# Ring slots at another offset, the last operands of h kept in the ring, weight sums and decodes at other steps, attention's head in another order

## The chip, the cores and the metric

The program runs on one core of a Trainium2 chip. TensorE (PE; its weight loads PEld) multiplies, VectorE (DVE), ScalarE (ACT) and GpSimd (POOL) work elementwise, SyncE (SP) issues transfers; ACT and POOL issue some too. The metric is the time of one execution in device microseconds; three runs of the kernel before gave 886.06, 886.5 and 888.85 us, a median of 886.5 us.

## The reference

Three stages, all float32. First a decayed linear attention over 4 batches of 8 heads, 768 positions of 64 features:

```
for t in range(S):
    state = gamma * state + k[t]^T v[t]          # 64 x 64 per head
    y[t]  = scale * q[t] state
```

Its output, 3072 tokens of 512 features, goes through `h = ((x @ w1) * (x @ w2)) @ w3; x = h @ w_out` (512 to 1024 to 1024 to 512), and then through `h = max(x @ w1, x @ w2, x @ w3); out = h @ w_out` (512 to 768 to 512). The weights reach the chip as 64-bit floats.

## The kernel before

**Operands and products.** Every 64-bit weight tile is fetched into one of three staging tiles (`stg`), decoded by a chain of short operations (ACT L113, POOL L115, DVE L136 and L138, ACT L145, then DVE L130 into `wraw`, or DVE L124 and ACT L126 for weights without sums) and split into a high and a low part, `w_q`. A product takes three matmuls of 128x512: high by high, high by low, low by high (L449 to L451, L559 to L561, L634 to L636, L690 to L692). ACT's cast and DVE's subtraction (`split_to`, L220 and L221) make the two parts of the moving operands in the same way.

**Seven products.** The products of stages B (x by w1 and w2, L449) and H (x by w1, w2, w3 of the last layer, L634) are done by a seven-product scheme on 2x2 blocks. One step q = 0..6 multiplies one operand (a sum of blocks of x, made by `op_pre`) with one weight set `w_q` (a sum of blocks of the weight, made by `weights`). A step of B has 24 matmuls, one of H has 18. B has 2 groups of 3 blocks of 7 steps (42), H has 3 columns j of 3 blocks (63). Operand s lies in ring slot `op_t[s % 4]`. In B's first group the operands are made in the ring and stored to DRAM (`opsp`); B's second group and H load them back, three steps ahead, with a DMA that POOL issues (L441, L538). Between B and H lie the merge of w3 with w_out (L498 to L500) and a stage M (L559), 24 steps, that makes x2, the input of H. H's operands are made by `gen(n, q)`: those of blocks 0 and 1 during M, those of block 2 during column 0 of H, at its steps 1, 2, 4, 5, 7, 8 and 10, through two tiles `gen0` and `gen1` and `opsp`.

**What sets the order.** The order of instructions is written out by hand; each engine runs its own in order. `Spread(jobs, slots)` deals out side jobs: at tick t it has run ceil(jobs x t / slots) of them. A tick comes after each quarter of a B step or third of an H step. One `step` is half a decode. `wgen(q)` writes `w_q` of the next group during the last block of the present one, one per step; its sums run on POOL (L197 to L199 at q = 2, L201 at q = 6), its split on ACT and DVE (L204, L205). In attention the decodes, a drain and the seven `wgen` are dealt over two ticks per chunk.

**Attention.** 24 chunks of 128 positions: `scores` (PE L293, then DVE's mask product L295 into `a`), `attn_av` (L311), `attn_st` (L322, state copied by ACT L326), `attn_in` (L302), `attn_ev` (DVE L331). `scale_v` (POOL L283) scales v in place two chunks ahead. A chunk is loaded in two halves, 512 KB each, into four slots `ck`.

Of the kernel before, what the change touches and what calls it, by code (L numbers as in the profile page):

```python
# [46 lines left out]
def fused_kernel(ctx: ExitStack, tc: tile.TileContext, ck, w12, w3t, wo1, w123, wo2, mask, gout, kdec, out):  # L47
# [107 lines left out]
    def drain():  # L155
        while loaded or fronts or mids or lows or pending or phase[0]:
            step()
        due_more()

    later = []  # L160

# [29 lines left out]
    def weights(raw, n):  # L191
        tmp = s_t[:, :n]

        def emit(q):
            r0, r1, r2, r3 = raw
            if q == 2:
                nc.gpsimd.tensor_tensor(out=tmp, in0=r2, in1=r3, op=ALU.add)  # L197
                nc.gpsimd.tensor_tensor(out=r2, in0=r2, in1=r0, op=ALU.subtract)
                nc.gpsimd.tensor_tensor(out=r0, in0=tmp, in1=r0, op=ALU.subtract)  # L199
            elif q == 6:  # L200
                nc.gpsimd.tensor_tensor(out=r1, in0=r1, in1=r0, op=ALU.subtract)  # L201
            src = (r0, r1, r0, r2, tmp, r3, r1)[q]
            w = wslot(q, n)
            nc.scalar.copy(out=w[:, 0], in_=src)  # L204
            nc.vector.tensor_tensor(out=w[:, 1], in0=src, in1=w[:, 0], op=ALU.subtract)  # L205

        return emit

    def raw_quads(n):
        return [wraw_t[0][:, i * n:(i + 1) * n] for i in range(4)]  # L210

    def op_slot(s):
        return op_t[s % 4][:, :].rearrange("p (h k n) -> p h k n", h=2, k=2)

    def view2(t):
        return t.rearrange("p (k n) -> p k n", k=2)
# [11 lines left out]
    def t_buf(n):  # L228
        return view2(work["T"][:, n % 2 * 1024:n % 2 * 1024 + 1024])

# [118 lines left out]

    with tc.manual_schedule():  # L350
        nc.sync.dma_start(out=mask_sb, in_=mask)
        load_half(0, 0)
        nc.sync.dma_start(out=kdec_sb, in_=kdec)
        load_half(0, 1)
        nc.sync.dma_start(out=gout_sb[:, 0], in_=gout[:, 0])
        load_half(1, 0)
        load_half(1, 1)
        for b in range(2):
            nc.gpsimd.memset(st_sb[b], 0.0)
# [12 lines left out]
        ops_b = {}  # L372
        side = Spread([step] * (4 * GA) + [drain] + [lambda q=q: wgen(q) for q in range(7)], 2 * (last - 3))
        for i in range(last + 1):
            attn_in(i)
            scores(i + 1)
            if i > 1:
                side.tick()
            attn_av(i)
            scale_v(i + 2)  # L380
            attn_st(i)
            attn_ev(i)
            if i > 1:
                side.tick()
            load_half(i + 4, 0)
            if i < 2:
                more()
                if i == 1:
                    more()
                    nc.sync.dma_start(out=gout_sb[:, 2:], in_=gout[:, 2:])  # L390
            load_half(i + 4, 1)
            if i == last - 2:
                op_split(0, quad_b(0)(0, 0))
# [4 lines left out]
        for nm in ("U", "C", "E", "T"):  # L398
            work[nm] = b_pl.tile([P, 2048], F32, name=nm)
        b_pl.tile([P, 8], F32, name="pad_b")  # L400
        op_split(1, quad_b(0)(1, 0))
# [3 lines left out]
        for g in range(KF // GA):  # L405
            if g == 0:
                wq += [lambda i=i, u=u: fetch_w12(i, u) for i in range(GA, KF) for u in range(2)]
                more(3)
                side = Spread([step] * (4 * GA), 2 * 28 + 4)
            else:  # L410
# [8 lines left out]
                more(3)  # L419
                side = Spread([step] * 32, 3 * 28)  # L420
            wgen = weights(raw_quads(1024), 1024)
# [121 lines left out]
        f_load(5)  # L543
        side = Spread([step] * (4 * GH), 18)
        wgen = weights(raw_quads(256 * GH), 256 * GH)
# [32 lines left out]
        g_st, g_pl = stage_pool("g")  # L578
        gen_t = [g_pl.tile([P, 2048], F32R, name=f"gen{z}") for z in range(2)]
        h_st, h_pl = stage_pool("h", "right")  # L580
# [16 lines left out]
        for j in range(GH):  # L597
# [3 lines left out]
            if j + 1 < GH:  # L601
                wq += [lambda w=w, u=u: fetch_w123(j + 1, w, u) for w in range(GH) for u in range(2)]
                side = Spread([step] * (4 * GH), 2 * 21 + 3)
            else:
                o_st, o_pl = stage_pool("o")
                wo2_sb = [o_pl.tile([P, 2, 512], F32R, name=f"wo2_{k}") for k in range(KH)]
                hop0 = o_pl.tile([P, 2, 1536], F32R, name="hop0")
                hop = [(hop0[:, 0], hop0[:, 1]), (w_t[0][:, :1536], w_t[1][:, :1536]), (w_t[2][:, :1536], w_t[3][:, :1536])]
                wq += [lambda k=k: fetch(wo2[k], None, wo2_sb[k][:, 0], wo2_sb[k][:, 1]) for k in range(KH)]
                side = Spread([step] * (2 * KH) + [drain], 2 * 21)  # L610
            more(3)
            wgen = weights(raw_quads(256 * GH), 256 * GH)
            for n in range(NB):
# [3 lines left out]
                for q in range(7):  # L617
                    s = 7 * blk + q
                    op_load(s + 3)
                    if s in (1, 2, 4, 5, 7, 8, 10):  # L620
                        gen(NB - 1, (1, 2, 4, 5, 7, 8, 10).index(s))
                    if j == GH - 1 and n == NB - 1 and q == 3:
# [4 lines left out]
                    which, first = ORDER[q]  # L627
                    x = op_slot(s)
                    w = wslot(q, 256 * GH).rearrange("p h (i k n) -> p h i k n", i=GH, k=2)
# [126 lines left out]
```

## Time and profile before

| | |
|---|---|
| median of 3 runs | 886.5 us |
| profiled execution, its own time | 884.03 us |
| its span, first to last instruction | 882.2 us |
| PE busy | 859.2 us (97%) |
| PE's weight loads busy | 709.7 us (80%) |
| DVE, ACT, POOL busy | 542.7, 344.2, 224.0 us |
| moved by DMA | 243.61 MB, 276 GB/s on average |

Busy times of PE contain modelled ends of pipelined matmuls, so that 97% says that PE rarely stands still, not how fast it goes. How fast it goes is read as the time of a stretch divided by its matmuls. All times below are microseconds from the start of the span.

### The profile page before, as it was taken

The numbers are of one execution on the slowest core, as the hardware profiler recorded it, in microseconds if no ns is written. First come the engines' busy times: TensorE is split into PE (matmuls) and PEld (weight loads), VectorE is DVE, ScalarE is ACT, GpSimd is POOL, SyncE is SP. The second block draws the span as 40 slices with busy tenths as digits, with TensorE's granted clock in tenths as the row PEclk, the third lists the DMA queues.
The fourth block names the chain that finished last, engine by engine and source line by source line (L and its number), as shares of the span: only waits on it lengthen the run. The fifth ranks groups of instructions, "written<-read, shape, count | busy, mean of one in ns | idle before, by whom it ended". The sixth has DMA issues, their size and how long they took to land. (4 is left out here: it accounts for less than half of the span.)

```text
span 882.2 us, 12037 instructions
## 1 busy us (share of the span) xinstructions
PE 859.2 (97%) x4614; PEld 709.7 (80%) x4614; DVE 542.7 (62%) x682; ACT 344.2 (39%) x530; POOL 224.0 (25%) x228
## 2 busy tenths in 40 slices
PE   8988999999999999999999999899999999999998
PEld 7877888888788888888888887688888778888886
DVE  2797969798485756752575577566656676351220
ACT  1333364543345343633554463343323342233231
POOL 2437215175242422100201232142214221000000
PEclk9999999999999999999999999999999999999999
DMA  9998277867799977453485599999998999965431
GB/s 336 408 379 266 97 291 281 345 251 284 279 324 355 323 255 278 143 210 120 170 286 242 211 402 411 417 330 344 375 325 269 314 359 343 305 203 178 153 118 63
DMA packets 63464, 243.61 MB, mean 276 GB/s; under 512 B 6320, under 2 KB 15664, under 8 KB 47152
## 3 DMA queue, kind: packets, MB, share of 16 engines
q1 hardware_dynamic: 45120, 132.23, 40.4%
q0 software_dynamic: 12096, 88.09, 28.3%
q10 hardware_dynamic: 6192, 22.55, 7.0%
q8 instruction: 36, 0.59, 0.3%
q14 instruction: 20, 0.16, 0.1%
HBM read 170.48 MB, written 72.35 MB: 275 GB/s over the span
## 5 line engine op out<-in xcount | busy, mean ns | idle before, releaser
L634 PE MATMUL bank<-op,w 128*128 128x512 f32 x378 | 149.6, 396 | 5.6 <-DVE m L652 2.0
L636 PE MATMUL bank<-op,w 128*128 128x512 f32 x378 | 148.2, 392 | 0.0
L635 PE MATMUL bank<-op,w 128*128 128x512 f32 x378 | 147.0, 389 | 0.0
L449 PE MATMUL bank<-op,w 128*128 128x512 f32 x336 | 132.5, 394 | 0.7 <-ACT U L454 0.7
L451 PE MATMUL bank<-op,w 128*128 128x512 f32 x336 | 131.6, 392 | 0.0
L450 PE MATMUL bank<-op,w 128*128 128x512 f32 x336 | 130.7, 389 | 0.0
L115 POOL TENSOR_SCALAR dec<-dec 128x512 f32<-128x512 f32 x64 | 46.6, 728 | 302.1 <-ACT dec L113 289.7
L634 PEld LDWEIGHTS bank<-op,w 128*128 128x128 f32 x378 | 71.0, 188 | 22.8 <-ACT E L643 3.1
L636 PEld LDWEIGHTS bank<-op,w 128*128 128x128 f32 x378 | 70.9, 188 | 16.6
L635 PEld LDWEIGHTS bank<-op,w 128*128 128x128 f32 x378 | 71.0, 188 | 15.5
L559 PE MATMUL bank<-op,w 128*128 128x512 f32 x192 | 75.6, 394 | 0.0
L561 PE MATMUL bank<-op,w 128*128 128x512 f32 x192 | 75.2, 392 | 0.0
L449 PEld LDWEIGHTS bank<-op,w 128*128 128x128 f32 x336 | 63.1, 188 | 14.6 <-ACT U L454 1.5
L451 PEld LDWEIGHTS bank<-op,w 128*128 128x128 f32 x336 | 63.1, 188 | 14.6
L560 PE MATMUL bank<-op,w 128*128 128x512 f32 x192 | 74.6, 389 | 0.0
L450 PEld LDWEIGHTS bank<-op,w 128*128 128x128 f32 x336 | 63.1, 188 | 13.8
L113 ACT ACTIVATE dec<-stg 128x512 f32<-128x512 f32 x64 | 42.5, 665 | 66.9 <-DMA stg<-in_wo_dram 32.1
L538 POOL DMA_DIRECT2D op<-opsp x63 | 34.6, 550 | 129.0 <-PE bank L636 103.7
L145 ACT ACTIVATE dec<-stg 128x512 int32<-128x512 uint32 x64 | 43.1, 673 | 56.8 <-DVE stg L138 56.6
L136 DVE TENSOR_SCALAR dec<-dec 128x512 int32<-128x512 int32 x64 | 37.0, 578 | 44.2 <-POOL dec L115 44.2
L138 DVE SCALAR_TENSOR_TENSOR stg<-stg,dec 128x512 int32<-128x512 int32 x64 | 46.7, 729 | 5.1 <-DVE dec L136 0.4
L465 POOL TENSOR_TENSOR C<-C,U 128x512 f32<-128x512 f32 x24 | 37.3, 1574 | 25.6 <-DVE C L464 25.6
(128 smaller groups left out, 1525.9 us busy)
## 6 DMA issues: line engine op xcount, KB each, us to landing
op<-opsp POOLq DMA_DIRECT2D x84, 1024.0 KB, 8.1
ck<-in_ck_dram SPq DMA_DIRECT2D x48, 512.0 KB, 7.1
opsp<-op SPq DMA_DIRECT2D x21, 1024.0 KB, 5.7
opsp<-w SPq DMA_DIRECT2D x14, 1024.0 KB, 4.9
stg<-in_w_dram ACTq DMA_DIRECT2D x19, 512.0 KB, 6.5
hsp<-m SPq DMA_DIRECT2D x36, 256.0 KB, 7.0
stg<-in_w3t_dram ACTq DMA_DIRECT2D x16, 512.0 KB, 4.3
stg<-in_w_dram SPq DMA_DIRECT2D x15, 512.0 KB, 9.6
```

The costliest lines, as they stand in the source:

```text
L115: nc.gpsimd.tensor_scalar(out=df, in0=df, scalar1=MAX_HI, scalar2=MIN_HI, op0=ALU.min, op1=ALU.max)
L138: nc.vector.scalar_tensor_tensor(out=top, in0=top, scalar=-0x40000000, in1=dec, op0=ALU.bitwise_and, op1=ALU.bitwise_or)
L145: nc.scalar.activation(out=dec, in_=low.bitcast(U32), func=ACT.Copy, scale=2.0 ** -29)
L449: nc.tensor.matmul(ps, wh, x[:, 0, k, :], start=first and k == 0, stop=False, skip_group_check=True)
L450: nc.tensor.matmul(ps, wh, x[:, 1, k, :], start=False, stop=False, skip_group_check=True)
L451: nc.tensor.matmul(ps, wl, x[:, 0, k, :], start=False, stop=k == 1, skip_group_check=True)
L559: nc.tensor.matmul(ps, wh, x[:, 0, k, :], start=kk == 0 and k == 0, stop=False)
L560: nc.tensor.matmul(ps, wh, x[:, 1, k, :], start=False, stop=False)
L561: nc.tensor.matmul(ps, wl, x[:, 0, k, :], start=False, stop=kk == 3 and k == 1)
L634: nc.tensor.matmul(ps, wh, x[:, 0, k, :], start=first and k == 0, stop=False, skip_group_check=True)
L635: nc.tensor.matmul(ps, wh, x[:, 1, k, :], start=False, stop=False, skip_group_check=True)
L636: nc.tensor.matmul(ps, wl, x[:, 0, k, :], start=False, stop=k == 1, skip_group_check=True)
```

## The change

1. **Offset.** Tile `T` shrinks from 2048 to 1536 columns and the pad behind it grows from 8 to 24. In the built program ring slots op1, op2 and op3 then start at bytes 173,952, 182,144 and 190,336 of a partition, multiples of 128; before it was 171,968, 180,160 and 188,352, 64 bytes past such a multiple. op0 starts at 94,336, a multiple of 128, in both. `t_buf` has one buffer where it had two. U, C, E and the `m` tiles move by the same kind of offset.
2. **Last operands of h.** In column 0 of H, `gen` makes operands 0, 1 and 2 of block 2 (at steps 1, 4 and 8) in three tiles that the matmuls of steps 14, 15 and 16 read directly. Operands 3 to 6 are made in their ring slots at steps 15 to 18 and stored from there. Operands 14 to 20 are not loaded in column 0.
3. **Weight sums.** `weights` runs the three sums right behind the split of q = 0 and the fourth behind that of q = 2. In attention the sets are dealt out as 0, 1, 5, 2, 3, 4, 6.
4. **Decodes.** Two or three empty jobs stand ahead of each group's decodes in B, M and H.
5. **Attention's head.** The first half chunk is loaded ahead of the mask and of `kdec`, `gout` behind chunk 1; `scores(1)` comes behind `attn_av(0)` and `attn_st(0)`.

```diff
@@ -157,6 +157,9 @@
+    def idle():
+        pass
@@ -193,24 +196,27 @@
             r0, r1, r2, r3 = raw
-            if q == 2:
-                nc.gpsimd.tensor_tensor(out=tmp, in0=r2, in1=r3, op=ALU.add)
-                nc.gpsimd.tensor_tensor(out=r2, in0=r2, in1=r0, op=ALU.subtract)
-                nc.gpsimd.tensor_tensor(out=r0, in0=tmp, in1=r0, op=ALU.subtract)
-            elif q == 6:
-                nc.gpsimd.tensor_tensor(out=r1, in0=r1, in1=r0, op=ALU.subtract)
             src = (r0, r1, r0, r2, tmp, r3, r1)[q]
...
             nc.vector.tensor_tensor(out=w[:, 1], in0=src, in1=w[:, 0], op=ALU.subtract)
+            if q == 0:
+                nc.gpsimd.tensor_tensor(out=tmp, in0=r2, in1=r3, op=ALU.add)
+                nc.gpsimd.tensor_tensor(out=r2, in0=r2, in1=r0, op=ALU.subtract)
+                nc.gpsimd.tensor_tensor(out=r0, in0=tmp, in1=r0, op=ALU.subtract)
+            elif q == 2:
+                nc.gpsimd.tensor_tensor(out=r1, in0=r1, in1=r0, op=ALU.subtract)
...
+    def quads4(o):
+        return o[:, :].rearrange("p (h k n) -> p h k n", h=2, k=2)
...
     def op_slot(s):
-        return op_t[s % 4][:, :].rearrange("p (h k n) -> p h k n", h=2, k=2)
+        return quads4(op_t[s % 4])
@@ -226,7 +232,7 @@
     def t_buf(n):
-        return view2(work["T"][:, n % 2 * 1024:n % 2 * 1024 + 1024])
+        return view2(work["T"][:, :1024])
@@ -348,13 +354,13 @@
     with tc.manual_schedule():
+        load_half(0, 0)
         nc.sync.dma_start(out=mask_sb, in_=mask)
-        load_half(0, 0)
+        load_half(0, 1)
         nc.sync.dma_start(out=kdec_sb, in_=kdec)
-        load_half(0, 1)
-        nc.sync.dma_start(out=gout_sb[:, 0], in_=gout[:, 0])
         load_half(1, 0)
         load_half(1, 1)
+        nc.sync.dma_start(out=gout_sb[:, 0], in_=gout[:, 0])
         for b in range(2):
@@ -370,15 +376,18 @@
         ops_b = {}
-        side = Spread([step] * (4 * GA) + [drain] + [lambda q=q: wgen(q) for q in range(7)], 2 * (last - 3))
+        side = Spread([step] * (4 * GA) + [drain] + [lambda q=q: wgen(q) for q in (0, 1, 5, 2, 3, 4, 6)], 2 * (last - 3))
         for i in range(last + 1):
             attn_in(i)
-            scores(i + 1)
+            if i:
+                scores(i + 1)
             if i > 1:
...
             attn_st(i)
+            if not i:
+                scores(i + 1)
             attn_ev(i)
@@ -396,8 +405,8 @@
         for nm in ("U", "C", "E", "T"):
-            work[nm] = b_pl.tile([P, 2048], F32, name=nm)
-        b_pl.tile([P, 8], F32, name="pad_b")
+            work[nm] = b_pl.tile([P, 1536 if nm == "T" else 2048], F32, name=nm)
+        b_pl.tile([P, 24], F32, name="pad_b")
         op_split(1, quad_b(0)(1, 0))
@@ -406,7 +415,7 @@
                 more(3)
-                side = Spread([step] * (4 * GA), 2 * 28 + 4)
+                side = Spread([idle] * 2 + [step] * (4 * GA), 2 * 28 + 4)
             else:
@@ -417,7 +426,7 @@
                 more(3)
-                side = Spread([step] * 32, 3 * 28)
+                side = Spread([idle] * 3 + [step] * 32, 3 * 28)
             wgen = weights(raw_quads(1024), 1024)
@@ -541,7 +550,7 @@
         f_load(5)
-        side = Spread([step] * (4 * GH), 18)
+        side = Spread([idle] * 2 + [step] * (4 * GH), 20)
         wgen = weights(raw_quads(256 * GH), 256 * GH)
@@ -576,7 +585,8 @@
         g_st, g_pl = stage_pool("g")
-        gen_t = [g_pl.tile([P, 2048], F32R, name=f"gen{z}") for z in range(2)]
+        gen_t = [g_pl.tile([P, 2048], F32R, name=f"gen{z}") for z in range(3)]
+        held = 7 * (NB - 1)
         h_st, h_pl = stage_pool("h", "right")
@@ -600,14 +610,14 @@
                 wq += [lambda w=w, u=u: fetch_w123(j + 1, w, u) for w in range(GH) for u in range(2)]
-                side = Spread([step] * (4 * GH), 2 * 21 + 3)
+                side = Spread([idle] * 2 + [step] * (4 * GH), 2 * 21 + 3)
             else:
...
                 wq += [lambda k=k: fetch(wo2[k], None, wo2_sb[k][:, 0], wo2_sb[k][:, 1]) for k in range(KH)]
-                side = Spread([step] * (2 * KH) + [drain], 2 * 21)
+                side = Spread([idle] * 2 + [step] * (2 * KH) + [drain], 2 * 21)
             more(3)
@@ -616,16 +626,26 @@
                     s = 7 * blk + q
-                    op_load(s + 3)
-                    if s in (1, 2, 4, 5, 7, 8, 10):
-                        gen(NB - 1, (1, 2, 4, 5, 7, 8, 10).index(s))
+                    if not held <= s + 3 < 7 * NB:
+                        op_load(s + 3)
+                    if s in (1, 4, 8):
+                        gen(NB - 1, (1, 4, 8).index(s))
+                    for d in (3, 2):
+                        t = s + d
+                        if held + len(gen_t) <= t < 7 * NB:
+                            qd = quad_h(NB - 1)
+                            if d == 3 and t > held + len(gen_t):
+                                op_pre(NB - 1, t % 7, qd)
+                            elif d == 2:
+                                op_split(t, op_src(NB - 1, t % 7, qd))
+                                store(opsp[NB - 1, t % 7], op_t[t % 4].bitcast(F32))
                     if j == GH - 1 and n == NB - 1 and q == 3:
...
                     which, first = ORDER[q]
-                    x = op_slot(s)
+                    x = quads4(gen_t[s - held] if held <= s < held + len(gen_t) else op_t[s % 4])
                     w = wslot(q, 256 * GH).rearrange("p h (i k n) -> p h i k n", i=GH, k=2)
...
                         ps = sets[which][p]

```

On POOL, around the weight sums of attention. `ck` is the chunk whose v is scaled, `wraw` the decoded weight, `s_t` a sum. Before:

```order
L283 TENSOR_TENSOR ck0_98<-ck0_98,kdec_110 128x512
L283 TENSOR_TENSOR ck1_99<-ck1_99,kdec_110 128x512
L283 TENSOR_TENSOR ck2_100<-ck2_100,kdec_110 128x512
L283 TENSOR_TENSOR ck3_101<-ck3_101,kdec_110 128x512
L197 TENSOR_TENSOR s_t_75<-wraw_94 128x1024
L198 TENSOR_TENSOR wraw_94<-wraw_94 128x1024
L199 TENSOR_TENSOR wraw_94<-s_t_75,wraw_94 128x1024
L283 TENSOR_TENSOR ck0_98<-ck0_98,kdec_110 128x512
```

Now:

```order
L289 TENSOR_TENSOR ck0_98<-ck0_98,kdec_110 128x512
L289 TENSOR_TENSOR ck1_99<-ck1_99,kdec_110 128x512
L204 TENSOR_TENSOR s_t_75<-wraw_94 128x1024
L205 TENSOR_TENSOR wraw_94<-wraw_94 128x1024
L206 TENSOR_TENSOR wraw_94<-s_t_75,wraw_94 128x1024
L289 TENSOR_TENSOR ck2_100<-ck2_100,kdec_110 128x512
L289 TENSOR_TENSOR ck3_101<-ck3_101,kdec_110 128x512
L289 TENSOR_TENSOR ck0_98<-ck0_98,kdec_110 128x512
```

The three sums have moved ahead of the scaling of two chunks (18 and 19).

On ACT, at the start of B's second group. `U` and `C` are copies of PSUM banks after q = 0 and q = 2, `dec<-stg` a decode of a weight that was just fetched. Before:

```order
L454 COPY U_1024<-bank4_81 128x512
L113 ACTIVATE dec0_66<-stg1_64 128x512
L454 COPY U_1024<-bank5_82 128x512
L454 COPY U_1024<-bank6_83 128x512
L145 ACTIVATE dec0_66<-stg1_64 128x512
L113 ACTIVATE dec1_67<-stg2_65 128x512
L454 COPY U_1024<-bank7_84 128x512
```

Now:

```order
L463 COPY U_1024<-bank4_81 128x512
L463 COPY U_1024<-bank5_82 128x512
L463 COPY U_1024<-bank6_83 128x512
L463 COPY U_1024<-bank7_84 128x512
L113 ACTIVATE dec0_66<-stg1_64 128x512
L467 COPY C_1025<-bank4_81 128x512
L467 COPY C_1025<-bank5_82 128x512
L145 ACTIVATE dec0_66<-stg1_64 128x512
```

The first decode has moved behind all four copies of q = 0 and the first place of q = 2.

On ACT, in column 0 of H, the casts into the tiles that `gen` writes, from step 3 on. Before:

```order
L145 ACTIVATE dec1_67<-stg2_65 128x512
L113 ACTIVATE dec0_66<-stg0_63 128x512
L82 DMA stg1_64<-in_w123_dram 128x512
L220 CAST gen0_3692<-T_1027 128x1024
L220 CAST gen1_3693<-x2_2_2912 128x1024
L648 COPY m02_3699<-bank4_81 128x512
L145 ACTIVATE dec0_66<-stg0_63 128x512
L113 ACTIVATE dec1_67<-stg1_64 128x512
```

Now:

```order
L226 CAST gen1_3693<-x2_2_2912 128x1024
L145 ACTIVATE dec1_67<-stg2_65 128x512
L113 ACTIVATE dec0_66<-stg0_63 128x512
L82 DMA stg1_64<-in_w123_dram 128x512
L668 COPY m02_3700<-bank4_81 128x512
L659 COPY U_1024<-bank7_84 128x512
L659 COPY U_1024<-bank0_77 128x512
L145 ACTIVATE dec0_66<-stg0_63 128x512
```

Two casts that wrote `gen0` and `gen1` for a second time are gone from this place; the copies of the next block stand where they stood.

## Rows read from the trace of the kernel before

**Rows 1.** The page's busy times: us, share of the span, instructions.

```profile
PE 859.2 (97%) x4614; PEld 709.7 (80%) x4614; DVE 542.7 (62%) x682; ACT 344.2 (39%) x530; POOL 224.0 (25%) x228
```

**Rows 2.** Waits of PE behind 106 us: us in total, times, longest.

```profile
PE bank L634 <- DVE m L652: 2.0, 2, 1.2
```

**Rows 3.** Waits of PE before 105 us.

```profile
PE bank L311 <- issue: 4.6, 2, 4.2
PE bank L293 <- DMA ck<-in_ck_dram: 3.6, 2, 2.7
```

**Rows 4.** Windows, PE: us, busy (matmuls), granted clock, DMA share, GB/s.

```profile
110.64:220.57 109.93, 109.93 (x481) 1.00 0.75 291
381.25:513.15 131.90, 131.90 (x578) 1.00 0.57 212
576.57:700.42 123.85, 123.85 (x541) 1.00 0.93 329
788.66:870.26 81.60, 81.60 (x362) 1.00 0.44 145
364.45:381.25 16.80, 16.80 (x73) 1.00 0.58 204
```

**Rows 5.** Windows, PE, of five stretches with pauses or beside them.

```profile
231.58:238.29 6.71, 6.05 (x26) 1.00 0.30 118
513.15:576.57 63.42, 58.87 (x254) 1.00 1.04 409
700.42:714.42 14.00, 12.92 (x55) 1.00 0.88 299
73.64:80.97 7.33, 7.33 (x114) 1.00 0.85 259
80.97:94.38 13.41, 9.22 (x114) 0.87 0.55 185
```

**Rows 6.** Timeline of ACT at B's second group: start, us, instruction, [idle before].

```profile
232.41 0.66 ACT L113 ACTIVATE dec<-stg 128x512 f32<-128x512 f32 x1 [9.26 <-DMA stg<-in_wo_dram]
```

**Rows 7.** Waits between 536 and 572 us, column 0 of H.

```profile
ACT gen L220 <- DMA opsp<-gen: 20.5, 3, 8.0
```

**Rows 8.** Timeline of attention's weight sums.

```profile
71.64 1.51 DVE L130 CUSTOM_DVE_ANT_0 wraw<-stg,dec 128x1024 uint16<-128x1024 uint16 x1
...
77.02 2.37 POOL L197 TENSOR_TENSOR s_t<-wraw 128x1024 f32<-128x1024 f32 x1
...
79.47 3.23 POOL L198 TENSOR_TENSOR wraw<-wraw 128x1024 f32<-128x1024 f32 x1
...
82.77 2.35 POOL L199 TENSOR_TENSOR wraw<-s_t,wraw 128x1024 f32<-128x1024 f32 x1
...
85.15 1.04 ACT L204 CAST w<-wraw 128x1024 fp32r<-128x1024 f32 x1 [5.43 <-POOL wraw L199]
```

**Rows 9.** Timeline of PE at the scores of chunk 6.

```profile
31.46 0.72 PE L293 MATMUL bank<-ck 64*128 64x128 f32 x8 [0.83 <-DMA ck<-in_ck_dram]
```

**Rows 10.** Window of attention: us, PE, PEld, DVE, ACT, POOL, clock, DMA share, GB/s.

```profile
20.00:40.00 20.00, 17.96 (x276) 16.30 (x274) 14.33 (x24) 8.16 (x17) 7.33 (x9) 1.00 1.02 417
```

**Rows 11.** Window of steps 14 to 20 of H, DVE: us, busy (instructions).

```profile
576.57:605.45 28.88, 22.16 (x26) 1.00 0.92 328
```

**Rows 12.** Timeline of DVE in columns 0 and 1 of H.

```profile
566.61 1.23 DVE L221 TENSOR_TENSOR gen<-x,gen 128x1024 fp32r<-128x1024 f32 x1 [6.21 <-ACT gen L220]
...
664.09 0.68 DVE L130 CUSTOM_DVE_ANT_0 wraw_h<-stg,dec 128x1024 uint16<-128x1024 uint16 x1
...
668.96 0.96 DVE L205 TENSOR_TENSOR w<-wraw_h,w 128x768 fp32r<-128x768 f32 x1 [4.18 <-PE bank L636]
...
672.47 2.50 DVE L654 TENSOR_TENSOR m<-m,U 128x512 f32<-128x512 f32 x1
```

**Rows 13.** Timeline of POOL in column 1 of H.

```profile
667.87 0.53 POOL L538 DMA_DIRECT2D op<-opsp  x1 [3.59 <-PE bank L636]
```

**Rows 14.** DMA issues between 640 and 700 us: KB each, us to landing.

```profile
op<-opsp POOLq DMA_DIRECT2D x13, 1024.0 KB, 6.6
```

## The prediction, made before the changed kernel ran

> **What bounds the kernel now.** I read four views in this order. The page's busy times say which engine to look at: PE, 97% of the span, all others far below [rows 1]. The list of PE's waits says how often it stands still: behind 106 us no one cause reaches more than the 2.0 us of [rows 2]; before 105 us, in attention, the two largest are 4.6 and 3.6 us [rows 3]. A busy PE can still be slow, so the third view is windows cut at step boundaries, each divided by its matmuls. The reader is to see in [rows 4] that one matmul of 128x512 takes 109.93 / 480 = 229.0 ns in B, 131.90 / 576 = 229.0 in M, 123.85 / 540 = 229.4 in H, but 81.60 / 360 = 226.7 in the last stage, and 16.80 / 72 = 233.3 in the merge's last three products (the counts in the rows hold one or two neighbours more). The clock is 1.00 in all five, so it is not the clock. Fourth come windows over the pauses [rows 5], and the timeline of the engine that was late there. The sum below is made against the profiled execution's 884.0 us; the median of the runs is 886.5, 2.5 more, which I add at the end.
>
> **Offset of the ring slots.** In B, M and H three of four moving operands lie in op1 to op3; in the merge's last three products the stationary operand does. These are the stages above 226.7 ns; the last stage reads none of the three slots. I take 226.7 as what a matmul costs with all slots at multiples of 128. B: 1008 matmuls x 2.35 ns = 2.4 us; M: 576 x 2.3 = 1.3; H: 1134 x 2.7 = 3.1; merge: 72 x 6.7 = 0.5. Together 7.2 us, all of it on PE and so on the end. Bounds: 0, if the place and not the offset counts, and 7.2, since the last stage shows no faster matmul. I take 7.2, because the rates split exactly by which slots are read. The Trainium skill (Advanced Engine Details and Errata, SBUF Cachelines) says that SBUF works in lines of 16 bytes and that accesses that fill their line run at full speed. By that rule an offset of 64 bytes, a multiple of 16, is as good as one of 128, and this term is 0; the rows do not settle it, since op1 to op3 differ from op0 in place as well.
>
> **First decode of a group.** In B's second group ACT sits 9.26 us in front of a decode whose weight has not landed [rows 6]; the copies of U stand behind it, and step 23 takes 6.71 us instead of 24 x 0.229 = 5.50 [rows 5]. Column 2 of H shows the same: steps 44 to 46 take 14.00 us against 54 x 0.2294 = 12.39. With the empty jobs the first decode comes at tick 8 and tick 6 instead of tick 1, behind all copies of q = 0. The weight lands when it did, so ACT waits for it at a place where no copy is due for a step. Gain 1.2 + 1.6 = 2.8 us; least 1.5, if ACT still blocks one copy. The decodes end at the same tick as before, so they crowd by one pair at most.
>
> **Column 0 of H.** Steps 0 to 13 take 63.42 us [rows 5] against 252 x 0.2294 = 57.8: 5.6 us are lost. ACT shows why: three casts into a `gen` tile wait up to 8.0 us, 20.5 in all, for the store of what was in it [rows 7]. Copies of PSUM banks, and decodes for which POOL's loads wait in turn, stand behind them. With three tiles each written once, no cast waits for a store. Column 0 also issues seven loads of 1 MB fewer, and its transfers are at 409 GB/s with a share of 1.04 [rows 5]. What comes instead: four splits and one difference on DVE in steps 14 to 20, 5 x 1.23 = 6.2 us [rows 12], on top of 22.2 busy of 28.9 [rows 11]. That makes 28.4 us, just inside, and a bank may be read one step late. The loads of operands 21 to 24 must wait for the stores from their slots; these are issued about two steps earlier. Bounds: 5.6 if all goes; 2.6 if DVE runs over by 3 us. I take 5.2.
>
> **Weight sums.** In B and M the sums start when the last raw weight is there, and POOL was free, so little changes: they run under PE's steps as before. T's single buffer costs nothing either: its last reader, the split of q = 5, comes four steps ahead of the next write, and both are in DVE's own order. In attention the cast of w2 waited 5.43 us for the third sum [rows 8]; DVE's split and then the mask product of chunk 19 queued behind it, and PE paused [rows 3]. Chunks 18 and 19 took 13.41 us where the two before took 7.33 [rows 5], so 6.1 us were lost, in part at a granted clock of 0.87 of full on average, that is with some of it at the lower level of 1.2 GHz. Now the sums stand right behind w0. They can start when the last raw weight is written, at 71.64 + 1.51 = 73.15, and take 2.37 + 3.23 + 2.35 = 7.95 us, to 81.1; w1 and w5 need none of them, and w2 comes later. But the scaling of chunk 18's v now stands behind them and ends near 82.1 (a scaling takes about 1 us), where chunk 18's products began at 80.97 (the second window's start). So PE waits 1.2 us there instead: gain 4.9. If each sum takes as long as the longest, 3.23 us, and the scaling 1.6, the wait is 3.5 us, and with the clock falling again the gain is 0.8. Above: 6.1. I take 4.7, near the rows' own durations. In column 1 of H the load for step 39 now stands behind the sums: they start at 664.8, the third waits for w0's split, which ends at 669.9 [rows 12], and takes 2.35 us [rows 8], so the load is issued near 672.3 instead of 667.87 [rows 13]. With 6.6 us to land [rows 14] it is there at 678.9, and step 39 begins 12.4 us (three steps of 4.13) behind the slot's release at about 667.4: it fits by 0.9. Cost 0 to 0.7; I take 0.2. The Trainium skill (SBUF — State Buffer, Who interferes with whom) says that a VectorE instruction with two SBUF inputs and a GpSimd instruction that reads SBUF lock each other out of a shared port. The trace agrees: a maximum of 128x512 takes 2.50 us at the time of a sum, a split of twice its size 1.23 without one [rows 12].
>
> **Attention's head.** PE paused 2.73 us for chunk 1, and chunk 2's scores would now start up to 1.4 us earlier. But the scores of chunk 6 wait for their data as they land [rows 9], with transfers at 417 GB/s and a share of 1.02 around it [rows 10], and the same bytes are queued ahead of them. What the head wins is waited for there. Gain between 0 and 1.4; I take 0.4, since the first large transfer is issued one place, some 0.45 us, earlier. A loss is excluded by that same later wait.
>
> **Sum.** 7.2 + 2.8 + 5.2 + 4.7 + 0.4 - 0.2 = 20.1 us. 884.0 - 20.1 = 863.9 for a profiled execution, 866.4 as a median of runs: forecast 866.
>
> **Rivals.** (1) The place, not the offset, makes three slots slow. For it: only op1 to op3 lie in the upper part of the partition. Against it: op0 and the last stage's tiles are spread far apart and equally fast. Then 20.1 - 7.2 = 12.9 us are won: 873.5. The rule of 16-byte lines would lead to the same time. (2) A wait takes the place of those removed: POOL's sums hold back two scalings in attention, and DVE is late in steps 14 to 20. For it: DVE at 28.4 of 28.9 us, with two-input operations at twice their time beside a sum [rows 12]. Against it: DVE's extra work needs only data that are there early. The gain falls by 4.7 - 0.8 = 3.9 and up to 2.6: some 6 us less, 872. Half of it gives 869. (3) Slower than before: the decodes start 5 to 8 ticks (about 8 us) later at six places (B twice, M, the three columns), and a group's last weights come late by as much, so that PE waits at each group's border. Six times 8 us is 48, less 20.1: 914. It decides from 20.1 / 6 = 3.4 us per place on. Against it: the dealer reaches the same last tick, and in column 1 the last raw weight is done 4.2 us before w0's split begins [rows 12].
>
> **Chances.** Forecast 0.55 (own range 863 to 870), rival 1 0.15, rival 2 0.26, rival 3 0.04. The range for 8 in 10 takes in rivals 1 and 2: 862 to 874.5. A difference under 0.3%, 2.7 us, is no change that this kernel's runs can tell. Faster needs only the forecast or rivals 1 and 2: 0.94. Same, for a slip that eats most of the gain: 0.02. Slower: 0.04.
>
> **What would show it.** Windows of B, M and H at 226.7 ns for a matmul confirm the offset; 229 there confirm rival 1. No cast into a `gen` tile waits for a store, steps 0 to 13 of H take 57.1 us (252 x 0.2267), steps 14 to 20 stay at 28.6; more means that DVE is late. No pause at steps 23 and 44. In attention PE waits once, 1 to 2 us, for POOL's scaling of chunk 18 and no longer 4.2 us for a mask product, and chunk 6 still waits for its transfer. A time over 875 would make this wrong, above all with weights late at group borders.

## The result and the profile after

The changed kernel takes 871.84 us in the median (870.96 to 872.08), the kernel before on the same chip 886.77; the ratio is 0.9826, 95% interval 0.9808 to 0.9844. The forecast was 866, its range 862 to 874.5. The profiled execution took 870.96 us with a span of 869.2, against 884.03 and 882.2: 13.1 us won, where the sum said 20.1. Between the medians 14.9 us are won; the profiled execution of the kernel before is faster than each of its four timed runs (886.06 to 888.85).

The windows of PE after the change, on step boundaries: B, M, H, the last stage, the merge's last three products; then steps 16 to 18 of B, steps 0 to 13 and 14 to 20 of H. Columns as in [rows 4].

```profile
107.79:189.39 81.60, 81.60 (x362) 1.00 0.73 288
376.52:507.08 130.56, 130.56 (x577) 1.00 0.55 202
616.48:738.88 122.40, 122.40 (x542) 1.00 0.94 336
767.44:849.04 81.60, 81.60 (x362) 1.00 0.50 164
360.20:376.52 16.32, 16.32 (x74) 1.00 0.50 180
189.39:207.85 18.46, 16.89 (x73) 1.00 0.57 194
507.08:567.39 60.31, 57.67 (x253) 1.00 0.95 374
567.39:595.95 28.56, 28.56 (x127) 1.00 0.55 209
```

By their matmuls the first five give 81.60/360, 130.56/576, 122.40/540, 81.60/360 and 16.32/72: 226.7 ns everywhere, where [rows 4] had 229.0, 229.4 and 233.3. Steps 14 to 20 fit exactly. Steps 16 to 18 of B should take 16.32 and take 2.14 more; steps 0 to 13 of H should take 57.12 and take 3.19 more, against the 5.6 lost in [rows 5].

The waits of PE behind 105 us, all of them, which answer to [rows 2], and the two largest before it, to [rows 3]. Each line gives us in total, times, longest.

```profile
PE bank L654 <- DMA op<-opsp: 2.6, 2, 1.9
PE bank L459 <- DVE op L227: 1.4, 1, 1.4
PE bank L458 <- DVE U L465: 0.2, 1, 0.2
```

```profile
PE bank L299 <- DMA ck<-in_ck_dram: 4.0, 5, 1.1
PE bank L317 <- POOL ck L289: 3.7, 2, 2.1
```

Steps 23 and 44 to 46 are no longer among them. New is, in B, a wait for a split into the ring. Late ring loads in column 0 are not new. The kernel before had one, ahead of step 12; it is the next line of the list that [rows 2] heads:

```profile
PE bank L634 <- DMA op<-opsp: 1.9, 1, 1.9
```

Now there are two, 0.75 us ahead of step 1 and 1.88 ahead of step 7. Before 105 us the wait of 4.2 us for a mask product is gone. PE waits five times for a chunk where it did twice, and twice for POOL's scaling (2.15 us at chunk 0, 1.58 at chunk 18) where it did once.

The sum, term by term, from the stage lengths of the two profiles (us won; a minus is a loss):

| term | forecast | measured |
|---|---|---|
| offset of the ring slots | 7.2 | 7.2 |
| first decode of a group | 2.8 | 2.8 |
| column 0 of H (5.6 lost before, 3.2 now) | 5.2 | 2.4 |
| attention, chunk 17 to 23 (26.52 us before, 22.57 now) | 4.7 | 4.0 |
| attention's head, to chunk 17 (77.31 before, 78.09 now), and its tail | 0.4 | -1.1 |
| weight sums in B | 0 | -2.1 |
| load in column 1 (step 39 is not late; 0.1 is lost at step 25) | -0.2 | -0.1 |

### The profile page after: what moved, and what is told of

It is laid out like the page before. It is cut to its first block, busy times and chain, and to the rows that moved or that the text cites. A ratio compares the mean times of both kernels' runs of the same rounds, so it can differ in the third digit from the quotient of the medians.

```text
span 869.2 us, 12019 instructions
## 1 busy us (share of the span) xinstructions
PE 847.4 (97%) x4614; PEld 706.2 (81%) x4614; DVE 543.2 (62%) x682; ACT 345.7 (40%) x530; POOL 223.4 (26%) x221
## 4 chain that ended last, share of the span: by engine, by line
PE 81%; DMA 7%; DVE 5%; issue 3%; POOL 1%; ACT 1%; SPq 0%; ACTq 0%; POOLq 0%; DVEq 0%
PE bank L654 9%; PE bank L656 9%; PE bank L655 9%; PE bank L459 7%; PE bank L460 7%; PE bank L458 7%; PE bank L570 4%; PE bank L568 4%; PE bank L569 4%; DMA ck<-in_ck_dram 4%; PE bank L711 4%; PE bank L710 4%; PE bank L712 4%; DMA op<-opsp 3%; PE bank L509 2%
## 5 line engine op out<-in xcount | busy, mean ns | idle before, releaser
L654 PE MATMUL bank<-op,w 128*128 128x512 f32 x360 | 140.3, 390 | 2.6 <-DMA op<-opsp 2.6
L656 PE MATMUL bank<-op,w 128*128 128x512 f32 x360 | 140.1, 389 | 0.0
L655 PE MATMUL bank<-op,w 128*128 128x512 f32 x360 | 140.1, 389 | 0.0
L459 PE MATMUL bank<-op,w 128*128 128x512 f32 x336 | 130.9, 389 | 1.4 <-DVE op L227 1.4
L458 PE MATMUL bank<-op,w 128*128 128x512 f32 x336 | 130.9, 390 | 0.2 <-DVE U L465 0.2
L460 PE MATMUL bank<-op,w 128*128 128x512 f32 x336 | 130.7, 389 | 0.0
L654 PEld LDWEIGHTS bank<-op,w 128*128 128x128 f32 x360 | 67.6, 188 | 17.8 <-DVE m L666 2.3
L656 PEld LDWEIGHTS bank<-op,w 128*128 128x128 f32 x360 | 67.6, 188 | 14.0
L655 PEld LDWEIGHTS bank<-op,w 128*128 128x128 f32 x360 | 67.6, 188 | 13.9
L459 PEld LDWEIGHTS bank<-op,w 128*128 128x128 f32 x336 | 63.1, 188 | 14.8 <-DVE op L227 1.8
L570 PE MATMUL bank<-op,w 128*128 128x512 f32 x192 | 74.7, 389 | 0.0
L568 PE MATMUL bank<-op,w 128*128 128x512 f32 x192 | 74.7, 389 | 0.0
L569 PE MATMUL bank<-op,w 128*128 128x512 f32 x192 | 74.7, 389 | 0.0
L458 PEld LDWEIGHTS bank<-op,w 128*128 128x128 f32 x336 | 63.1, 188 | 13.9 <-issue 0.8
L460 PEld LDWEIGHTS bank<-op,w 128*128 128x128 f32 x336 | 63.1, 188 | 13.1
L136 DVE TENSOR_SCALAR dec<-dec 128x512 int32<-128x512 int32 x64 | 35.0, 548 | 45.4 <-POOL dec L115 45.4
L547 POOL DMA_DIRECT2D op<-opsp x56 | 31.0, 554 | 109.6 <-PE bank L656 85.1
L474 POOL TENSOR_TENSOR C<-C,U 128x512 f32<-128x512 f32 x24 | 37.8, 1595 | 20.1 <-DVE C L473 20.1
```

Source lines behind the costliest of these rows:

```text
L458: nc.tensor.matmul(ps, wh, x[:, 0, k, :], start=first and k == 0, stop=False, skip_group_check=True)
L459: nc.tensor.matmul(ps, wh, x[:, 1, k, :], start=False, stop=False, skip_group_check=True)
L460: nc.tensor.matmul(ps, wl, x[:, 0, k, :], start=False, stop=k == 1, skip_group_check=True)
L568: nc.tensor.matmul(ps, wh, x[:, 0, k, :], start=kk == 0 and k == 0, stop=False)
L569: nc.tensor.matmul(ps, wh, x[:, 1, k, :], start=False, stop=False)
L570: nc.tensor.matmul(ps, wl, x[:, 0, k, :], start=False, stop=kk == 3 and k == 1)
```

## The experiments

A time without a range is a single run. Ten runs of one kernel below lie as far as 6.9 us apart, so a single run is read by the lengths of its stages and steps.

**Offset alone.** The kernel before, with the ring moved by 64 bytes.

```diff
-        b_pl.tile([P, 8], F32, name="pad_b")
+        b_pl.tile([P, 24], F32, name="pad_b")
```

> The kernel before with one edit: the pad behind the ring's pool is 24 elements instead of 8, so op1 to op3 and U, C, E, T lie 64 bytes lower, at multiples of 128 bytes; all else is as before. Offset theory: every unstalled step takes 5440 ns (24 matmuls) or 4080 ns (18) in all four slots, as in the changed kernel, and the time falls by 7.2 us, to 879.5 (879 to 881, if transfers take some of it back). Rival, the place or another edit (gen tiles, T's single buffer) made the matmuls faster: steps stay at 5493 to 5510 ns in slots 1 to 3 and the time stays within 1 us of 886.8.

All unstalled steps take 5440 and 4080 ns: it is the offset. Windows of B, M and H:

```profile
111.44:193.04 81.60, 81.60 (x362) 1.00 0.74 289
381.95:512.51 130.56, 130.56 (x577) 1.00 0.60 220
576.51:698.91 122.40, 122.40 (x542) 1.00 0.93 334
```

But the time is 881.32 us (877.32 to 884.21) against 886.03, ratio 0.9947 (0.9927 to 0.9968): some 4.7 us, not 7.2. Part is given back where faster steps meet data that arrive when they did. Its waits of PE show it:

```profile
PE bank L634 <- DVE m L652: 2.5, 2, 1.7
PE bank L634 <- DMA op<-opsp: 2.3, 2, 1.9
PE bank L449 <- ACT U L454: 1.9, 2, 1.7
PE bank L449 <- DMA op<-opsp: 1.2, 1, 1.2
```

Step 23 is 2.5 us too long, behind the copies of U, where it was 1.2, and column 0 loses 6.9 instead of 5.6. Steps 29 and 30 of B lose 1.5 to a late ring load; the changed kernel loses as much there in one of its two profiles, and nothing in the other. The pause at steps 44 to 46 is gone here too, although the decodes stand as before.

**Three offsets at once.** The changed kernel with op1, op2, op3 at 32, 64 and 96 bytes past a multiple of 128, op0 at 0.

```diff
+        for i in range(1, 4):
+            b_pl.tile([P, 8], F32, name=f"shift{i}")
             op_t.append(b_pl.tile([P, 2048], F32R, name=f"op{i}"))
```

> The changed kernel with 8 spare elements ahead of each of op1, op2 and op3 and 8 behind: op0 lies at 0, op1 at 32, op2 at 64, op3 at 96 bytes past a multiple of 128; U, C, E, T stay at multiples of 128. Theory A, whatever is not at a multiple of 128 pays alike: steps in slots 1, 2 and 3 all take 5490 to 5510 ns, slot 0 5440. Theory B, the cost hangs on the distance: the three slots differ by more than 10 ns from each other. Rival, lines of 16 bytes: all four at 5440. The whole by A: 871 + 7 = 878.

Four steps of B, which read op2, op3, op0 and op1 in turn:

```profile
114.75:120.36 5.61, 5.61 (x26) 1.00 1.01 415
120.36:125.95 5.59, 5.59 (x25) 1.00 0.99 407
125.95:131.42 5.47, 5.47 (x26) 1.00 0.51 198
131.42:137.03 5.61, 5.61 (x25) 1.00 0.97 377
```

By the starts of their matmuls the medians are 5603, 5596, 5464 and 5617 ns: for op1 to op3 that is 6.5 to 7.4 ns a matmul more than 226.7, some three times what 64 bytes cost in the kernel before. Neither theory holds as put. The three are nearly alike, as theory A has it, but at three times its price. They differ by up to 21 ns, more than theory B's 10, but in the kernel before slot 1 takes 17 ns more than slots 2 and 3 as well, with all three at 64 bytes. So it isn't shown that the price hangs on the distance, and the distance alone doesn't set it: at 64 bytes a step takes 5493 to 5510 ns there and 5603 here, with the slot 1920 bytes higher. What sets it stays open. The whole, 884.84, is one run.

Slot 0 lies at a multiple of 128 in both kernels, and yet its steps take 5464 ns here and 5490 in the kernel before. The excess sits in the first matmuls of the step (there the first ten, 232 ns in the mean); from then on each takes 226.7, and where all four slots lie at multiples of 128, all do. So the excess comes only behind a step whose operand is off; why, no run shows.

The rival drew on the 16-byte lines of the Trainium skill (Advanced Engine Details and Errata, SBUF Cachelines), by which any multiple of 16 would do. These operands don't bear it out: 32, 64 and 96 are multiples of 16, and all three cost time.

**Without the empty jobs.**

```diff
-                side = Spread([idle] * 3 + [step] * 32, 3 * 28)
+                side = Spread([step] * 32, 3 * 28)
...
```

The same is done at the other four places.

> The changed kernel without the empty jobs ahead of the decodes (B, M and H); all else as changed. Theory: the first decode of a group again waits in ScalarE ahead of the copies of U; step 23 takes 1.2 us or more longer than 5440 ns, steps 44 to 46 of H's third column 1.6 us in all; 2.8 to 4 us longer than the changed kernel, 873.8 to 875. The waits end when the weights land, and steps are now shorter, so they may be longer than before. Rival: the empty jobs did nothing, the faster steps alone removed the pauses: steps 23 and 44 to 46 stay at 5440 and 4080 ns.

879.18 us, 8.2 more than the changed kernel: 4.5 in B, 3.0 in H. ACT in B's second group, and windows of PE over step 22, step 23 and a part of step 23:

```profile
233.55 0.66 ACT L113 ACTIVATE dec<-stg 128x512 f32<-128x512 f32 x1 [12.49 <-DMA stg<-in_wo_dram]
234.11 1.06 ACT L463 COPY U<-bank 128x512 f32<-128x512 f32 x2
```

```profile
224.29:229.73 5.44, 5.44 (x25) 1.00 1.01 371
229.73:240.33 10.60, 7.12 (x26) 0.84 0.50 179
234.73:237.40 2.67, 2.67 (x6) 0.50 0.06 23
```

ACT waits for the weight, the copies of U stand behind it, and PE waits for these: 3.48 us of step 23. Then PE runs at a granted clock of 0.50, the level of 1.2 GHz, for 2.7 us. Step 23 is 5.2 us too long where the kernel before lost 1.2, so in B the empty jobs are worth more than their term. In H it is less plain: steps 23 and 44 lose 1.9 us, most of the rest of the 3.0 lies in steps 0 to 13, and the loss of 1.6 at steps 44 to 46 of the kernel before is not there again.

**B's fourth sum later.**

```diff
-            elif q == 2:
+            elif q == fourth:    # 5 in B's first group
```

> The changed kernel with the fourth weight sum of B's first group at q = 5 instead of q = 2; the rest as it is. Theory: the fourth sum, at 198.12 us beside the split of step 18's operand, stretches that split to 3.42 us and makes steps 16 to 18 late by 2.15 us in all; moved away, the three steps take 5440 ns each (within 0.3 us in all), B is 2.1 us shorter and the whole near 868.8. Rival: the first three sums and the decodes alone fill VectorE; steps 16 to 18 stay 1.5 us or more late in all.

870.57 us (one run). Steps 16 to 18 take 16.81 us instead of 18.46: 1.65 of the 2.14 are back, and 0.49 stay, in steps 16 and 17, beside the first three sums. So the theory holds for the larger part and its rival falls. VectorE in the changed kernel, and in this one:

```profile
191.03 3.42 DVE L227 TENSOR_TENSOR op<-xr,op 128x1024 fp32r<-128x1024 f32 x1
199.03 3.42 DVE L227 TENSOR_TENSOR op<-xr,op 128x1024 fp32r<-128x1024 f32 x1
```

```profile
199.50 1.22 DVE L227 TENSOR_TENSOR op<-xr,op 128x1024 fp32r<-128x1024 f32 x1
216.20 2.41 POOL L208 TENSOR_TENSOR wraw<-wraw 128x1024 f32<-128x1024 f32 x1
```

The split at 199.03, and here at 199.50, is that of step 18's operand: beside the fourth sum it takes 3.42 us, without it 1.22 (the one at 191.03 stays, beside the first three). At 216.20 the sum makes no step late. B as a whole won only 1.0, since step 30 was 0.67 us late in this run; other profiles of the same code there differ by up to 1.4.

**Attention's sums back.** The changed kernel with the sums ahead of the cast of w2 in attention alone, weights in the order 0 to 6.

```diff
+            if old and q == 2:       # the three sums, as before the change
...
+            elif old and q == 6:     # the fourth
...
```

> The changed kernel with attention's weight sums where they were (before the cast of w2, weights in the order 0 to 6); all else as changed. Theory, the sums alone gave what attention won: the stretch from the products of chunk 17 to those of chunk 23 goes from 22.57 us back to 26.5, with a pause of about 4 us before the mask product of chunk 19; the whole near 875. Rival, the new head or run-to-run differences of transfers gave it: the stretch stays under 24 us.

875.42 us; chunk 17 to 23 takes 27.48 us instead of 22.57, and 26.52 before, so the rival falls. The old pause on PE is back, before the products of chunk 19 (the column in brackets is the wait ahead):

```profile
84.38 1.16 PE L307 MATMUL bank<-ck 64*128 64x128 f32 x16
89.45 1.02 PE L325 MATMUL bank<-a,ck 128*64 128x128 f32 x3 [3.90 <-issue]
```

**Attention's sums behind one more scaling.** GpSimd in the changed kernel has the three sums and the scaling of chunks 18 to 20 behind them, answering to [rows 8]; the split of w0 on VectorE, for which the third sum waits; then PE's wait for the scaling.

```profile
73.18 2.38 POOL L204 TENSOR_TENSOR s_t<-wraw 128x1024 f32<-128x1024 f32 x1 [2.77 <-DVE wraw L130]
75.63 2.36 POOL L205 TENSOR_TENSOR wraw<-wraw 128x1024 f32<-128x1024 f32 x1
79.22 2.37 POOL L206 TENSOR_TENSOR wraw<-s_t,wraw 128x1024 f32<-128x1024 f32 x1 [1.23 <-DVE w L202]
81.53 5.02 POOL L289 TENSOR_TENSOR ck<-ck,kdec 128x512 f32<-128x512 f32 x3
```

```profile
75.73 3.35 DVE L202 TENSOR_TENSOR w<-wraw,w 128x1024 fp32r<-128x1024 f32 x1
```

```profile
83.62 0.77 PE L317 MATMUL bank<-a,ck 128*64 128x128 f32 x10 [1.58 <-POOL ck L289]
```

```diff
-        ... for q in (0, 1, 5, 2, 3, 4, 6)], 2 * (last - 3))
+        ... for q in (0, 1, 5, 2, 3, 4, 6)], 2 * (last - 3) + 1)
```

> The changed kernel with one slot more for attention's dealer, so that the three sums stand behind the scaling of chunk 18's v instead of ahead of it; nothing else. Theory: chunk 18's products start without a wait; from the products of chunk 17 to those of chunk 23 it takes 22.57 - 1.5 = 21.0 us or a little more. Rival: the scaling of chunk 19 (or the mask product) is late instead by as much: 22.3 us or more.

Chunk 17 to 23 takes 21.97 us: 0.6 won, not 1.5. Chunk 18 no longer waits, and chunk 19's scaling is there in time: the rival as put falls too. But everything behind came nearer, and PE now waits 0.7 us each before chunks 19 and 23, the first time for VectorE:

```profile
81.91 2.46 DVE L202 TENSOR_TENSOR w<-wraw,w 128x1024 fp32r<-128x1024 f32 x1
84.30 0.68 DVE L337 TENSOR_TENSOR xr<-bank,gout 128x512 f32<-128x512 f32 x1
```

The eviction at 84.30, which frees the bank that PE needs, stands behind a weight's split, stretched by the sums. The whole, 872.98, holds a longer wait in column 0 of H, which the edit doesn't touch.

**The old head.** The changed kernel with the first loads and scores in their old order.

```diff
...
-            if i:
-                scores(i + 1)
+            scores(i + 1)
...
```

> The changed kernel with the head of attention as before the change; all else as changed. Theory: chunk 6's scores begin 1 us or more later than 30.05 us, but the load of chunk 9's second half is issued by 35 us, chunks 12 to 14 wait for no transfer, and chunk 17's products begin at 77.3 to 78.1 us instead of 78.09 in the changed kernel (78.6 as a median of its variants). Rival: chunks 12 to 14 wait as well and chunk 17 begins after 78.6 us.

Chunk 6 begins at 31.50 us instead of 30.05, chunk 17 at 77.83 instead of 78.09; the whole is 871.26. SP's waits between 27 and 45 us, in the changed kernel and in this one:

```profile
SPq L270 <- DMA stg<-in_w_dram: 6.7, 1, 6.7
SPq L270 <- PE bank L328: 6.3, 3, 2.2
```

```profile
SPq L270 <- PE bank L328: 9.0, 4, 2.3
SPq L270 <- PE bank L308: 3.2, 5, 0.6
```

With the new head SP stands 6.7 us in front of the load of chunk 9's second half until a weight has landed that this load has nothing to do with. In the compiled program the transfers issued by SP and ACT take eight completion semaphores in turn, and these two have the same one. It goes out at 36.26 us, where PE had freed the place near 32.8 (1.64 us behind the start of chunk 5's products, as with the old head); so some 3.4 of the 6.7 us are the semaphore's. The loads behind it are late too, and chunks 12 to 14 wait 2.2 us for their data:

```profile
PE bank L299 <- DMA ck<-in_ck_dram: 2.2, 3, 1.1
```

This is no accident of one profile: PE waits 1.9 to 2.4 us there in nine of the ten profiles with the new head, and in none of the four with the old. Over the same profiles chunk 6 begins at 30.05 to 31.71 us with the new head and at 31.14 to 31.50 with the old, and chunk 17 begins at 77.7 to 80.2 us with the new head (ten, median 78.7) and at 77.3 to 78.7 with the old (four, median 77.9). The new head wins nothing; that it loses 0.8 is within the spread.

**Column 0 as before the change, and the gen stores later.**

```diff
-        gen_t = [g_pl.tile([P, 2048], F32R, name=f"gen{z}") for z in range(3)]
+        gen_t = [g_pl.tile([P, 2048], F32R, name=f"gen{z}") for z in range(2)]
...
-                    if s in (1, 4, 8):
+                    if s in (1, 2, 4, 5, 7, 8, 10):
```

```diff
-            store(opsp[n, q], g.bitcast(F32), 1)
+            store(opsp[n, q], g.bitcast(F32), wait)    # 11 for column 0
```

> The changed kernel with column 0 of H as before the change: two gen tiles, all seven operands of the last block stored and loaded again. Theory of the prediction: casts into gen tiles wait for stores and steps 0 to 13 lose 5 us or more; H is 3 us or more longer than 260.36. Rival, column 0 is bound by transfers either way (412 to 419 GB/s from 507 to 558 us): the seven loads that the change drops come behind step 10, so steps 0 to 10 lose about as much (2 to 3 us) with either, and what the change wins lies in steps 11 to 20.

> The changed kernel with the three gen tiles of column 0 of H stored ten steps later (near steps 12, 15 and 19 instead of 2, 5 and 9). Theory, transfers are full: they run at 412 to 419 GB/s from 507 to 558 us, and two stores of 1 MB less before step 7 free about 5 us of transfer time, so the wait of 1.88 us before step 7 of H goes, and H is 1.9 us shorter (whole near 869.1). Rival, the load of step 7's operand is late because GpSimd issues it behind a decode that waits for ScalarE: the wait stays at 1 us or more. The wait of 0.75 us before step 1 stays in both, since no gen store is out yet.

With the old column 0, H takes 267.68 us instead of 260.36 (whole 880.87); steps 0 to 13 take 65.88, steps 0 to 10 alone 4.0 more than in the changed kernel. ACT's waits for the stores are back:

```profile
ACT gen L226 <- DMA opsp<-gen: 18.2, 5, 7.3
```

The rival, that the gain lies behind step 10, falls. With faster steps the old column would lose 8.8 us and not 5.6, so its change is worth 5.6 there and still leaves 3.2.

What is left lies in steps 0, 1, 6 and 7, at the two late ring loads, while the transfers are full. The changed kernel in two stretches of column 0 and behind it (PE, PEld, DVE, ACT, POOL busy, clock, DMA share, GB/s):

```profile
517.00:527.00 10.00, 10.00 (x46) 8.29 (x45) 8.59 (x11) 6.44 (x11) 3.48 (x5) 1.00 1.05 419
527.00:537.00 10.00, 9.87 (x44) 7.80 (x42) 9.81 (x17) 1.83 (x3) 1.71 (x3) 1.00 1.04 415
557.00:583.00 26.00, 26.00 (x116) 21.56 (x115) 19.91 (x26) 11.41 (x17) 9.78 (x5) 1.00 0.34 132
```

With the stores later, the wait before step 7 is gone (steps 0 to 13: 58.20), as the theory has it; the decode that stands ahead of step 7's load on GpSimd is still there and costs nothing. So the wait before step 7 is the transfers'; the one before step 1 stays, as expected. But the last store now goes out among the stores from the ring slots. GpSimd, which must wait for one of these before it loads for column 1, waits 8.2 us where it waits 4.5 in the changed kernel. A load is 2.8 us late at step 24, the clock falls to 0.84 in the mean around it, and H takes 263.81. GpSimd's wait, and PE around step 24:

```profile
POOL op L547 <- DMA opsp<-op: 8.2, 1, 8.2
```

```profile
606.96:617.72 10.76, 7.95 (x29) 0.84 1.07 415
```

The whole is 875.76.

**Repairs together.** The fourth sum at q = 5, the dealer's extra slot, M's third sum behind q = 1, the gen stores at steps 11 to 13; then the same with the old head.

```diff
+            if q == third:     # 1 in M
...
+                        gen(NB - 1, (1, 4, 8).index(s), {1: 10, 4: 8, 8: 5}[s])
```

> The changed kernel with four edits: the fourth sum of B's first group at q = 5; M's third sum behind its q = 1, so that the first ring load of H stands ahead of it; the stores of the three gen tiles at steps 11 to 13 of H, where hardly any transfer runs; attention's dealer with one slot more, so that GpSimd scales chunk 18 ahead of the sums. Theory, each repairs the wait that the trace of the changed kernel shows: 1.7 us in B (the fourth sum's part), 1.5 us at chunk 18, 0.7 us before step 1 and 1.9 us before step 7 of H; together 5.8 us, 866 in the median. Rival, the waits move: the transfers that are late at steps 1 and 7 are late elsewhere, and scaling of chunk 19 waits instead of chunk 18; then at most 2 us are won, 870 or more.

> The kernel of the run combined with the head of attention as it was before the change (order of the first loads, scores of chunk 1 ahead of chunk 0's products). Theory: the new head buys nothing; in the eight profiles that have it chunk 17's products begin at 77.7 to 79.3 us (median 78.6), in the two with the old head at 77.3 and 78.05, since the load of chunk 9's second half is issued near 36.5 us instead of 34 behind a weight transfer and chunks 12 to 14 wait. So chunk 17 begins near 77.7 and the time is 0.5 to 1 us under that of combined, 868; as a ratio to before 0.981. Rival: the 1.4 us that the new head wins by chunk 6 are kept; then chunk 17 begins at 79 or later and the time is 869.5 or more.

> The changed kernel once more, as it is, so that it stands beside the combined kernel on the same chip. Theory: combined wins 3 us over it, in its absolute time (868.8 against 871.8): 871.5 to 872.5 here. Rival: only the chip differed, since both gave the same ratio to the kernel before; then the two are within 1 us of each other.

combined: 868.84 us (868.29 to 870.18), 0.9827 (0.9803 to 0.9851) of before; B is 229.09, H 259.37. With the old head 867.98 (866.23 to 869.69), 0.9803 (0.9772 to 0.9834). The changed kernel beside it on the same chip takes 872.15 (871.79 to 873.26), 0.9852 (0.9812 to 0.9892). So the repairs with the old head beat the changed kernel by 4.2 us, and no run of the one reaches the other; of this the head's share can't be told, and chunk 17 begins at 78.7 in that profile. Of the 5.8 us expected from the four edits, combined wins 3.3 over the changed kernel beside it. In column 0 the wait before step 1 shrinks to 0.24 us, and the one before step 7 moves to step 13, 1.15 us in combined, and 2.0 with the old head:

```profile
PE bank L652 <- DMA op<-opsp: 2.6, 3, 2.0
```

## Why the prediction was right, and where it failed

The direction and the range were right, and the largest term exact. The sum was 7.0 us too high against the profile, in four places, and the forecast 5.8 too low against the median. The time, 871.84, lies outside the forecast's own range of 863 to 870; the range for 8 in 10 held because it took in the rivals. It lies next to the 872 of rival 2, whose general statement holds: waits took the place of those removed. But its two places are not where the time was lost: POOL's sums cost 0.7 us and not 3.9, and DVE is not late in steps 14 to 20. So that number is met by luck.

**Offset of the ring slots.** Right: 226.7 ns in every slot, the merge too, and the ring moved alone gives the same steps. Rival 1, the place instead of the offset, falls, though the place takes part in the price. The reason given, that the rates split exactly by which slots are read, holds for stages and not for steps: slot 0 took 5490 ns in the kernel before. The term came out because the stages' means hold that excess too. What the prediction didn't see is that the 7.2 us are only kept where nothing else arrives late: alone, 4.7 of them remain.

**First decode of a group.** The 2.8 us are gone. For the 1.2 in B the run without the empty jobs shows that they did it; with the faster steps 5.2 would have been lost there. For the 1.6 at steps 44 to 46 of H it isn't shown: they are gone with the offset alone as well.

**Column 0.** The step "no cast waits for a store" is right for the `gen` tiles, and so is the load on VectorE: steps 14 to 20 take 28.56, and that half of rival 2 falls. Wrong is what was drawn from it, that steps 0 to 13 take 57.1 and 5.2 us are won. The prediction noted the transfers at 409 GB/s with a share of 1.04 and set nothing for them; that a ring load was 1.9 us late there, in its own list of waits, it booked on the casts. The steps became shorter, and two ring loads still come late; with them 3.2 us are lost. For the one ahead of step 7 the later stores show that it is the full transfers. The one ahead of step 1 shrinks where GpSimd issues the load ahead of a sum.

**Weight sums in attention.** Right in place and nearly in size: 4.0 for 4.7. PE waits 1.58 us for the scaling of chunk 18 where 1.2 was taken, since the third sum waits 1.23 us for the split of w0, which takes 3.35 beside a sum. That is 0.4 of the 0.7; the rest was not traced.

**Weight sums in B.** Here the step "POOL was free, so little changes" failed: 2.1 us. That POOL is free says nothing of VectorE, which has a split due in each of these steps, and whose split takes 3.42 us beside a sum instead of 1.22. The prediction cited that lockout for column 1 and did not apply it in B.

**Attention's head.** The step "what the head wins is waited for there" looked to chunk 6 only; "a loss is excluded" is refuted in its reason: the order of issues also decides which transfers share a semaphore, and chunks 12 to 14 waited besides chunk 6, which still waits 0.9 us for its transfer, as foreseen. Of the loss of 1.1 in the table 0.8 lies ahead of chunk 17. Between 0.4 and -0.8 nothing can be told in the time.

## What to carry to other kernels

A gain per instruction, as by alignment, is only kept where weights and operands arrive earlier too: look for the waits that a faster engine will meet, above all where transfers already have a share of 1. Before work is moved to a free GpSimd, read what VectorE has due in the same microseconds. A reordered load is judged by all loads behind it, not by the first.

## What was not expected of the hardware

A matmul of 128x512 takes 226.7 ns with its operand at a multiple of 128 bytes in the partition, 229.0 in slots 64 bytes past it, and 233.2 to 234.0 in slots 32, 64 and 96 bytes past it that lie some 1.9 KB higher; with a stationary operand 64 bytes past it, 233.3. In the kernel before, the first ten matmuls of a step in the aligned slot took 232 ns in the mean, behind a step whose operand was not aligned. A split on VectorE takes 3.42 us beside a sum on GpSimd and 1.22 without. A load of SP stood behind a transfer of ACT with which it had nothing in common but the completion semaphore, and went out some 3.4 us late by it.
